# A Fourier transform fused into a leaky-ReLU MLP: moving the last chunk's sums to VectorE and splitting one weight conversion

## The chip, the cores and the metric

The kernel runs on one core of a Trainium2 chip. A core has five engines that each work through their own queue of instructions and wait for one another by semaphores: TensorE (matmuls, PE in the profile, with its weight loads as PEld), VectorE (DVE), ScalarE (ACT), GpSimd (POOL), and SyncE (SP), which here only issues transfers between HBM and the on-chip memory SBUF. TensorE writes its results to the eight banks of a second memory, PSUM. The metric is the time of one execution on the device in microseconds, taken as the median of three runs.

## The reference

```python
def _attn_ref(x):                       # x: (8, 3008, 256)
    X = np.fft.fft(x, axis=1)
    X = np.fft.fft(X, axis=2)
    return X.real.astype(np.float32)

def _moe_ref(x, w_in, w_out):           # x: (24064, 256), w_in: (256, 2048), w_out: (2048, 256)
    h = x @ w_in
    g = np.maximum(0.01 * h, h)
    return (g @ w_out).astype(np.float32)
```

The real part of a two-dimensional Fourier transform over sequence and features is taken for each of eight batches. Its 24064 rows then go through an MLP with a hidden layer of 2048 and a leaky ReLU. The weights are given in float64.

## The kernel before

Everything is computed in fp32. The transform along the features is folded into `w_in`, so that one set of weights `wf` stands for both. The transform along the sequence is made of sums and differences on VectorE and GpSimd (called folds) and a few matmuls with cosine and sine tables (`dft`, lines 489 to 524 and 691 to 701). Its result for one batch and one parity of the frequencies is a unit; there are 16 units. The float64 weights are turned into fp32 by bit operations (class `Weights`, lines 551 to 601). `begin` cuts out mantissa and exponent, `mantissa` (line 591, one VectorE instruction) adds the low word, and `end` (lines 600 and 601, two VectorE instructions) puts sign and exponent in. `w_out` comes in eight parts, o to o7.

The columns of the output are worked on in chunks. Two first pieces take a plain way (lines 881 to 931). The other columns make 31 chunks (t from 0 to 30), the class `Chunk`. A chunk of up to 378 pairs of columns goes through these stages:

- `up` (line 1090): for each of 16 blocks f of the hidden layer, one matmul into a cosine bank and one into a sine bank. ScalarE copies the cosine part (line 1099), VectorE makes sum and difference of the two (line 1106, a pair of instructions, which also empties the sine bank), and ScalarE applies the leaky ReLU (line 1360).
- The product with `w_out` is a block matrix product by a scheme with fewer multiplications. It has 28 sums of hidden blocks (`SUMS`, `Chunk.sum`, line 1123, one instruction of 128 x 752 numbers each), 18 sums of weights made once (`W_SUMS`, `sum_weights`, on GpSimd, line 661), 26 products of four matmuls each (`PRODUCTS`, line 1140; a matmul appears as two in the profile), and 34 combinations of the products (`COMBINED`, line 1184) on VectorE, some of them after ScalarE has copied a product out of PSUM (line 1156). Eight of the combinations are results, which SyncE stores.

The products go in turn into three banks, `sum_psa` to `sum_psc`. A product takes a bank only after the combinations that read its former content (`leave`, line 1168).

The order of the instructions on each engine is written out by `rest` (line 1272). It makes a list of events, each with a time in steps; a chunk has 16 steps, one for each block f, and the events are issued in the order of those times. Chunk t starts at step 16 t. Its ups come at 1.20 and on, its sum i at `SUMS_AT[i]`, and its products from step 18.1 on at 6.5 matmuls a step. So one chunk's products run beside the next chunk's ups, and after the last chunk's ups only its sums, products and combinations are left. At whole steps `start_work` issues other work, and the function `some` gives out folds and combinations from their queues, up to an amount that `now[0]` scales.

Ten sums of each chunk are on VectorE (`BY_VECTOR`) and 18 on GpSimd. In the last chunk the sums with i % 3 == 2 are on VectorE also, which makes 17 there and 11 on GpSimd:

```python
every[t].sum(i, nc.vector if i in BY_VECTOR or t == count - 1 and i % 3 == 2 else None)   # line 1346
```

A sum on GpSimd is given one more wait: `wait_for_gate` (line 990) makes it wait for the last instruction before it on VectorE that has both its operands in SBUF, although it uses no result of that instruction.

The last part of `w_out`, o7, is converted at step 2 of the first chunk, and the weight sums that read it follow:

```python
if r == 2:                      # line 1383
    convert_on(o7, None)        # mantissa, then end
    sum_weights(2)
    sum_weights(3)
```

Of the kernel before, what the change touches and what calls it, by code (L numbers as in the profile page):

```python
# [46 lines left out]
PLAIN = 2  # L47
EARLY = 14
FIRST_DOWN = 18.1
RF = 126  # L50
FIRST_SHARE = 1.0
DIRECT = (11, 13)
WORK_FROM = 14
FOLDS_FROM = 16
# [34 lines left out]
NA = 24  # L89

SUMS_AT = [14.51, 15.26, 16.05, 16.0, 16.74, 17.24, 17.74, 18.73, 18.48, 19.22, 19.47, 20.71, 20.32, 21.56, 22.06, 22.67, 22.04, 24.14, 24.64, 25.38, 25.37, 27.17, 27.22, 28.21, 29.08, 30.06, 30.17, 31.54]
UP_FROM, DOWN_FROM, PER_STEP, LATER = 1.20, 18.10, 6.5, 0
BY_VECTOR = (0, 3, 6, 8, 9, 12, 16, 17, 21, 25, )
ON_POOL, ON_VECTOR, AHEAD, X_AHEAD, TRANSFORM_FROM, TURNS = 1.20, 1.20, 1, 2, 8, 2
SLOTS, RS, SS, PARTS = 28, 191, 764, 24

# [184 lines left out]
def tile_fnet_leaky_relu(  # L281
# [15 lines left out]
    nc = tc.nc  # L297
# [137 lines left out]
    class Rows:  # L435
# [3 lines left out]
        def __init__(self, src, scratch, part, c):  # L439
            self.src, self.scratch, self.part, self.c = src[0:ROWS], scratch, part, c  # L440
            self.places = PLACES[c] if part else range(16)
# [170 lines left out]
    def convert_on(old, new):  # L612

        old.mantissa()
        if new is not None:
            new.begin()
        return old.end()
# [380 lines left out]
    class Slots:  # L998
# [3 lines left out]
        def __init__(self):  # L1002
            self.under = {SLOTS + i: {4 * RF * i // SS, (4 * RF * (i + 1) - 1) // SS} for i in range(16)}
            self.free = set(range(SLOTS)) - set().union(*self.under.values())
# [23 lines left out]
        def place(self, i, n):  # L1028
            if i >= SLOTS:
                return block_sb[:, (i - SLOTS) * 4 * RF : (i - SLOTS + 1) * 4 * RF].rearrange("p (g n) -> p g n", g=4)[:, :, 0:n]  # L1030
            return block_sb[:, i * SS : i * SS + 4 * RS].rearrange("p (g n) -> p g n", g=4)[:, :, 0:n]

        def row(self, r, g, n):
            if r[0] >= SLOTS:
                all_of = block_sb[:, 0 : 64 * RF].rearrange("p (i n) -> p i n", n=4 * RF)
                return all_of[:, r[0] - SLOTS : r[-1] + 1 - SLOTS, g * RF : g * RF + n]
            all_of = block_sb.rearrange("p (i n) -> p i n", n=SS)
# [206 lines left out]
    def work():  # L1244

        yield WORK_FROM, 0
        load_x(1, 0)
        yield FOLDS_FROM, 0  # L1250
        folds_of_x(0)
        for u in range(1, len(units) - 1):
            b, c = units[u]
            if c == 0:
                yield step_of(u, 0), 0
                load_x(b + 1, 1)
                yield 0, X_AHEAD
                folds_of_x(1)
                fold_halves_of_x()
                yield from transform(u + 1)  # L1260
            else:
                yield step_of(u, 0), 0
                if b + 1 < B:
                    load_x(b + 1, 0)
                    yield 0, X_AHEAD
                    folds_of_x(0)
                yield step_of(u, TRANSFORM_FROM), 0
                yield from transform(u + 1)

    every, waiting = [], []  # L1270

    def rest():

        count = len(chunk)
        every.extend(Chunk(t) for t in range(count))
        events = []
        for t in range(count):
            for f in range(NF):
                events.append((16 * t + UP_FROM + f, 3, t, f))
            for i, s in enumerate(SUMS_AT):  # L1280
                events.append((16 * t + s + LATER, 1, t, i))
            for m in range(4 * len(PRODUCTS)):
                events.append((16 * t + (DOWN_FROM if t else FIRST_DOWN) + m / PER_STEP, 2, t, m))
        for r in range(16 * count + 18):
            events.append((r + 0.01, 0, r // 16, r % 16))
        events.sort()
        rings["up"] = [0, [cos_ps[1], sin_ps[1]]]
        rings["sum"] = [0, sums_ps]
        rings["ev"], rings["e0"] = [0, [ev_sb]], [0, [e0_sb]]
        ups = [(t, f) for t in range(count) for f in range(NF)]  # L1290

        def seed(at):
            if at < len(ups):
                every[ups[at][0]].seed(ups[at][1])

        def seed_next(at):

            if at < EARLY:
                seed(at + 1)
            if at + 2 > EARLY:  # L1300
                seed(at + 2)

        us, now = [0.0, 0.0], [1.0]

        def some(pool):

            us[pool], us[1 - pool] = min(us[pool], 0.3) + (ON_VECTOR, ON_POOL)[pool] * now[0], us[1 - pool] - 100.0
            for part in every:
                part.make_some(us)
            folds.emit(us)  # L1310
            us[1 - pool] += 100.0

        todo, until, empty = work(), 0, -1

        def go_on(step):
            nonlocal until, empty
            while not folds.queue:
                if empty < 0:
                    empty = step
                if step < max(until, empty + after[0]):  # L1320
                    return
                got = next(todo, None)
                if got is None:
                    until = 10**6
                    return
                until, after[0] = got
                empty = -1

        after = [0]
        seed(0)  # L1330
        for _, kind, t, i in events:
            if kind == 0:
                start_work(16 * t + i)
                now[0] = FIRST_SHARE if 16 * t + i < 34 else 1.0
                if 0 < t < count:
                    rings["dft"] = [0, [misc_ps]]
                if t == count and waiting:
                    for to in waiting.pop():
                        nc.scalar.activation(to, to, ACT.Lrelu)
                go_on(16 * t + i)  # L1340
                some(1)
                if t >= count:
                    folds.emit_copies()
                    some(0)
            elif kind == 1:
                every[t].sum(i, nc.vector if i in BY_VECTOR or t == count - 1 and i % 3 == 2 else None)
            elif kind == 2:
                every[t].product(*divmod(i, 4))
                if t == count - 1:
                    for pool in (0, 1, 0, 1):  # L1350
                        some(pool)
            else:
                if i == 0 and t > 0 and every[t].u > every[t - 1].u:
                    assert t < 2 or transformed[0] >= every[t].u and not folds.queue, (t, transformed, len(folds.queue))
                part = every[t]
                made = part.up(i)
                seed_next(16 * t + i)
                folds.emit_copies()
                for to in sum(waiting, []):
                    nc.scalar.activation(to, to, ACT.Lrelu)  # L1360
                waiting[:] = [part.hidden(*made)]
                some(0)
        while any(part.open for part in every):
            some(0)
            some(1)
# [6 lines left out]
    def start_work(r):  # L1372


        if r == 0:
            convert_on(o6, o7)
        if r in PLAIN_UP:
            raised(*steps[PLAIN_UP[r]])
            activate(*steps[PLAIN_UP[r]], later=waiting)
        if r in PLAIN_DOWN:  # L1380
            at, half = PLAIN_DOWN[r]
            down_plain(*steps[at], halves=(half,))
        if r == 2:
            convert_on(o7, None)
            sum_weights(2)
            sum_weights(3)
        if r in (5, 7):
            part = (r - 5) // 2
            fold_halves(t, part, 0, slice(0, 2 * FI))
            evens.append(Direct(t[:, part, 0, :, part * P : (part + 1) * P], part, even_tables[part], 0))  # L1390
        if r in (8, 10):
            evens[(r - 8) // 2].fold_odd(t[:, (r - 8) // 2, 1, 0:2, 0:P])
        if r == 9:
            rings["dft"] = rings["up"]
            nyq_t = nyquist_tile()
            made = butterfly(nyquist_halves(nyq_t, 0), B, 0, 0)
            made[0](even_rows(nyq_of[0], B))
            made[1](odd_rows(nyq_of[0], B))
            store_nyquist(0, nyq_t)
            spread(1)  # L1400
        if r in DIRECT:
            dft_direct(DIRECT.index(r))
# [9 lines left out]
    with tc.manual_schedule(engines={mybir.EngineType.DVE, mybir.EngineType.PE, mybir.EngineType.SP}):  # L1412
        with tc.manual_schedule(engines={mybir.EngineType.Pool, mybir.EngineType.Activation}):
# [9 lines left out]
            t = xt[:, 0 : 8 * FI * D].rearrange("p (h m c d) -> p h m c d", h=2, m=2, c=2 * FI)  # L1423
# [85 lines left out]
        with tc.manual_schedule(engines={mybir.EngineType.Pool, mybir.EngineType.Activation}):  # L1509
# [35 lines left out]
            o6, o7 = load_w_out(6), load_w_out(7, now=False)  # L1545
# [61 lines left out]
```

## Time and profile before

| | |
|---|---|
| median of 3 runs | 1833.05 us (1833.03 to 1833.87) |
| the profiled execution's own time | 1834.63 us |
| its span, first to last instruction | 1832.8 us |
| TensorE busy | 1818.5 us, 99% |
| VectorE busy | 1546.2 us, 84% |
| ScalarE busy | 1124.6 us, 61% |
| GpSimd busy | 1101.7 us, 60% |
| mean granted TensorE clock | 0.998 |
| sums on GpSimd (line 1123) | 551, 1955 ns each on average |
| sums on VectorE (line 1123) | 317, 1299 ns each on average |

The profile is of one execution. A row of the timeline gives start, duration, engine, line, operation, what is written and read, the shape and the number of instructions, and in brackets how long the engine was idle before it and whose result ended that. "L1140" is a line of the code. A mean of a group mixes instructions that ran freely with those that stood still during their execution. The granted clock is the share of full speed that TensorE was allowed.

### The profile page before, as it was taken

Reading aid. Unit: us, or ns where it says so; the run is one execution under the profiler, and the core shown is the slowest. Engines: PE = TensorE matmul, PEld = TensorE weight load, DVE = VectorE, ACT = ScalarE, POOL = GpSimd, SP = SyncE. Lnnn points to the kernel's source line nnn. Section 1 sums busy time; section 2 is a strip of 40 time slices with the busy share of each in tenths; the row PEclk is TensorE's granted clock in tenths of the full one; section 3 lists DMA queues with packets and bytes.
Section 4 is the critical chain, followed back from the end, with each engine's and each line's share of the span. In section 5 each row is a group of like instructions: output and inputs, shape, how many; then the busy total and the mean of one; then the engine's idle time right before and its main releaser. Section 6 shows DMA issues by size and latency. Waiting matters only on the chain.

```text
span 1832.8 us, 27088 instructions
## 1 busy us (share of the span) xinstructions
PE 1818.5 (99%) x9424; PEld 1547.3 (84%) x9424; DVE 1546.2 (84%) x3212; ACT 1124.6 (61%) x2298; POOL 1101.7 (60%) x595
## 2 busy tenths in 40 slices
PE   9999999999999999999999999999999999999998
PEld 7887888888888888888888888888888888888887
DVE  8979898897888978899787988879898798788776
ACT  4558666675666756576565766557666675565650
POOL 0244666565666666666665666666566665766664
PEclk9999999999999999999999999999999999999999
DMA  6312021202102011021101112111021100100000
GB/s 235 118 39 98 28 70 34 72 14 68 33 28 72 23 63 30 29 70 35 63 18 54 46 33 72 33 53 30 28 70 35 65 16 30 27 30 18 14 9 30
DMA packets 65897, 88.61 MB, mean 48 GB/s; under 512 B 10064, under 2 KB 53456, under 8 KB 65760
## 3 DMA queue, kind: packets, MB, share of 16 engines
q1 hardware_dynamic: 65616, 86.88, 14.6%
q8 instruction: 74, 1.21, 0.3%
q14 instruction: 63, 0.52, 0.1%
q10 hardware_dynamic: 144, 0.00, 0.0%
HBM read 62.12 MB, written 24.72 MB: 47 GB/s over the span
## 4 chain that ended last, share of the span: by engine, by line
PE 96%; DVE 2%; POOL 1%; issue 1%; POOLq 0%; ACT 0%; DVEq 0%
PE sum_psc L1140 21%; PE sum_psa L1140 17%; PE sum_psb L1140 16%; PE cos_psa L1093 9%; PE sin_psa L1093 8%; PE cos_psb L1093 8%; PE sin_psb L1093 8%; PE dft_ps L699 3%; PE sum_psa L925 1%; PE dft_ps L925 1%; PE sum_psb L925 1%; PE sum_psc L925 1%; DVE part L1184 1%; PE sum_psa L1410 1%; POOL block L1123 1%
## 5 line engine op out<-in xcount | busy, mean ns | idle before, releaser
L1123 POOL TENSOR_TENSOR block<-block 128x752 f32<-128x752 f32 (+2 forms) x551 | 1070.0, 1955 | 638.8 <-DVE xt L946 178.7
L1360 ACT ACTIVATE block<-block 128x376 f32<-128x376 f32 (+5 forms) x718 | 426.4, 623 | 3.2 <-DVE block L1106 2.5
L1123 DVE TENSOR_TENSOR block<-block 128x752 f32<-128x752 f32 (+2 forms) x317 | 411.1, 1299 | 5.9 <-POOL block L1123 5.7
L1106 DVE TENSOR_TENSOR block<-cos,sin_psa 128x376 f32<-128x376 f32 (+2 forms) x510 | 250.9, 533 | 143.5 <-PE sin_psa L1093 139.9
L1140 PEld LDWEIGHTS sum_psc<-block,wt 128*128 128x128 f32 x1736 | 291.2, 190 | 47.1 <-issue 1.8
L1140 PE MATMUL sum_psc<-block,wt 128*128 128x188 f32 (+2 forms) x1736 | 329.2, 322 | 1.7 <-DVE part L1184 1.7
L1106 DVE TENSOR_TENSOR block<-cos,sin_psb 128x376 f32<-128x376 f32 (+2 forms) x482 | 240.2, 539 | 104.2 <-PE sin_psb L1093 103.0
L1140 PE MATMUL sum_psa<-block,wt 128*128 128x188 f32 (+2 forms) x1736 | 312.8, 321 | 0.4 <-POOL block L1123 0.4
L1140 PEld LDWEIGHTS sum_psa<-block,wt 128*128 128x128 f32 x1736 | 283.4, 189 | 23.5 <-POOL block L1123 0.7
L1099 ACT COPY cos<-cos_psa 128x376 f32<-128x376 f32 (+2 forms) x255 | 119.0, 467 | 250.6 <-PE cos_psa L1093 247.8
L1099 ACT COPY cos<-cos_psb 128x376 f32<-128x376 f32 (+2 forms) x241 | 113.6, 471 | 210.4 <-PE cos_psb L1093 210.3
L1093 PE MATMUL sin_psa<-mixs,wf 128*128 128x376 f32 (+2 forms) x510 | 199.9, 473 | 1.1 <-DVE block L1106 1.1
L1093 PE MATMUL cos_psa<-mixc,wf 128*128 128x376 f32 (+2 forms) x510 | 199.8, 473 | 0.5 <-ACT cos_psa L1088 0.5
L1184 DVE TENSOR_TENSOR part<-part 128x188 f32<-128x188 f32 (+2 forms) x465 | 189.8, 445 | 2.8 <-ACT part L1156 1.0
L1093 PE MATMUL sin_psb<-mixs,wf 128*128 128x376 f32 (+2 forms) x482 | 191.5, 479 | 0.0
L1093 PE MATMUL cos_psb<-mixc,wf 128*128 128x376 f32 (+2 forms) x482 | 191.4, 478 | 0.0
L1140 PE MATMUL sum_psb<-block,wo 128*128 128x188 f32 (+2 forms) x992 | 187.6, 321 | 0.0
L1140 PEld LDWEIGHTS sum_psb<-block,wo 128*128 128x128 f32 x992 | 165.3, 189 | 22.8
L1140 PEld LDWEIGHTS sum_psb<-block,wt 128*128 128x128 f32 x992 | 163.5, 189 | 22.8
L1140 PE MATMUL sum_psb<-block,wt 128*128 128x188 f32 (+2 forms) x992 | 176.8, 321 | 0.0
L1088 ACT ACTIVATE cos_psa<-nb,wn 128x376 f32<-128x376 f32 (+2 forms) x255 | 146.0, 572 | 8.4
L1093 PEld LDWEIGHTS sin_psa<-mixs,wf 128*128 128x128 f32 x510 | 96.4, 189 | 63.2 <-DVE block L1106 1.7
(212 smaller groups left out, 1954.3 us busy)
## 6 DMA issues: line engine op xcount, KB each, us to landing
xt<-in_x_dram SPq DMA_DIRECT2D x28, 1024.0 KB, 5.5
out_dram<-part SPq DMA_DIRECT2D x176, 94.0 KB, 1.7
out_dram<-part SPq DMA_DIRECT2D x64, 94.5 KB, 1.7
tabe<-in_seq_tab_dram SPq DMA_DIRECT2D x29, 190.0 KB, 2.5
nb<-nyq_dram SPq DMA_DIRECT2D x23, 188.0 KB, 3.8
block<-in_w_in_dram SPq DMA_DIRECT2D x8, 512.0 KB, 5.5
block<-in_w_out_dram SPq DMA_DIRECT2D x8, 512.0 KB, 4.6
xt<-in_first_x_dram SPq DMA_DIRECT2D x4, 768.0 KB, 8.2
```

The source lines that it names most:

```text
L699: nc.tensor.matmul(o, lhsT=still, rhs=moving, start=(i == 0), stop=(i == 3), skip_group_check=True)
L925: nc.tensor.matmul(sums[j][d][:, r * n : (r + 1) * n], lhsT=wo[:, fs[h] // 4, fs[h] % 4, d], rhs=a[r][h], start=(f == 0 and r == 0 and h = ...
L1088: nc.scalar.activation(cos_ps[self.half(f)][:, 0 : self.w], columns_of(nb_sb, self.u, self.j, self.w), ACT.Copy, scale=wn[:, f : f + 1])
L1093: nc.tensor.matmul(bank[:, 0 : self.w], lhsT=wf[:, i, f * P : (f + 1) * P], rhs=columns_of(mix_sb[i], self.u, self.j, self.w), start=(i == ...
L1099: nc.scalar.copy(copy, cos[:, 0 : self.w])
L1106: nc.vector.tensor_tensor(block.row(to, g, self.n), x, y, op=op)
L1123: ins = (engine or nc.gpsimd).tensor_tensor(self.value(16 + i), xa, ya, op=ALU.add if sign > 0 else ALU.subtract)
L1140: nc.tensor.matmul(to, lhsT=weight(w)[:, g], rhs=self.value(v)[:, g], start=(first and at == 0), stop=(last and g == 3), skip_group_check= ...
L1184: ins = nc.vector.tensor_tensor(part_of[self.copy[v]][:, 0:n], xa, ya, op=ALU.add if sign > 0 else ALU.subtract)
L1360: nc.scalar.activation(to, to, ACT.Lrelu)
L1410: nc.tensor.matmul(pt[:, 0:columns], lhsT=blank[:, 0:P], rhs=blank[:, 0:columns], start=True, stop=True)
```

## The change

- In the last chunk (t = 30) all 28 sums are on VectorE, the eleven of GpSimd included (`LAST_ON_POOL` is empty). In the other chunks `ON_GPSIMD` is the complement of the former `BY_VECTOR`: nothing moves.
- The last chunk's sums are issued one step sooner, but those that were due after step 17.05 not before that point, and those that were due before it at their old place.
- The conversion of o7 is split. Its `mantissa` is issued at step 1 of the first chunk, its `end` at step 3, with the weight sums that follow.
- The amount that `some` gives out is scaled by 0.9 before step 34 and by 1.2 from there to step 48; it was 1.0.
- `LATER` (which was 0) goes, and `FIRST_PER` has the value of `PER_STEP`.

```diff
-FIRST_SHARE = 1.0
+FIRST_PER = 6.5
+O7_AT = (1, 3)
+SHARES = (0.9, 1.2)
...
-UP_FROM, DOWN_FROM, PER_STEP, LATER = 1.20, 18.10, 6.5, 0
-BY_VECTOR = (0, 3, 6, 8, 9, 12, 16, 17, 21, 25, )
+UP_FROM, DOWN_FROM, PER_STEP = 1.20, 18.10, 6.5
+ON_GPSIMD = (1, 2, 4, 5, 7, 10, 11, 13, 14, 15, 18, 19, 20, 22, 23, 24, 26, 27)
+LAST_ON_POOL = ()
+LAST_SOONER = 1.0
...
             for i, s in enumerate(SUMS_AT):
-                events.append((16 * t + s + LATER, 1, t, i))
+                events.append((16 * t + (s if t < count - 1 else max(s - LAST_SOONER, min(s, 17.05))), 1, t, i))
             for m in range(4 * len(PRODUCTS)):
-                events.append((16 * t + (DOWN_FROM if t else FIRST_DOWN) + m / PER_STEP, 2, t, m))
+                events.append((16 * t + (DOWN_FROM + m / PER_STEP if t else FIRST_DOWN + m / FIRST_PER), 2, t, m))
...
-                now[0] = FIRST_SHARE if 16 * t + i < 34 else 1.0
+                now[0] = SHARES[0] if 16 * t + i < 34 else SHARES[1] if 16 * t + i < 48 else 1.0
...
-                every[t].sum(i, nc.vector if i in BY_VECTOR or t == count - 1 and i % 3 == 2 else None)
+                every[t].sum(i, None if i in (LAST_ON_POOL if t == count - 1 else ON_GPSIMD) else nc.vector)
...
-        if r == 2:
-            convert_on(o7, None)
+        if r == O7_AT[0]:
+            o7.mantissa()
+        if r == O7_AT[1]:
+            o7.end()
             sum_weights(2)
             sum_weights(3)
```

## The prediction

> **What bounds the kernel now.** I read the busy row first, then TensorE's idle time in order of time, then the engines that end it, last the granted clock.
>
> ```profile
> PE 1818.5 (99%) x9424; PEld 1547.3 (84%) x9424; DVE 1546.2 (84%) x3212; ACT 1124.6 (61%) x2298; POOL 1101.7 (60%) x595
> ```
>
> TensorE sets the time; a change is worth what it gives back of the 14.3 us in which TensorE isn't busy, and of any time at a lower clock. The waits by window leave three places: about 103 us, 181 to 189 us, and the last 41 us. From 192 to 1776 us TensorE shows no wait at all. TensorE in the tail (start, duration, what, idle before it):
>
> ```profile
> 1790.67 1.44 PE L1140 MATMUL sum_psb<-block,wo 128*128 128x188 f32 x8
> 1795.66 2.87 PE L1140 MATMUL sum_psc<-block,wo 128*128 128x188 f32 x8 [3.56 <-POOL block L1123]
> 1798.33 4.45 PE L1140 MATMUL sum_psc<-block,wt 128*128 128x188 f32 x16
> ...
> 1813.38 1.54 PE L1140 MATMUL sum_psa<-block,wt 128*128 128x188 f32 x8 [0.40 <-POOL block L1123]
> ...
> 1826.49 1.54 PE L1140 MATMUL sum_psc<-block,wo 128*128 128x188 f32 x8
> ```
>
> Eight matmuls normally take 1.275 us from start to start, so the group at 1795.66 was due at 1791.95. Besides the 3.7 us of waiting, its own eight take 2.67 and the next sixteen 4.29 instead of 2.55: half speed. The same stretch by windows (PE, PEld, DVE, ACT, POOL, then the granted clock):
>
> ```profile
> 1792.00:1796.00 4.00, 0.44 (x2) 0.34 (x2) 1.98 (x3) 0.54 (x2) 4.00 (x2) 0.88 0.17 55
> 1796.00:1804.00 8.00, 8.00 (x33) 8.00 (x33) 5.79 (x3) 0.00 (x0) 5.52 (x3) 0.63 0.00 0
> ```
>
> A mean of 0.88 over 4 us is 0.97 us at one half, 0.63 over 8 us is 5.9: the clock was halved for 6.9 us, from 1795.03, 2.9 us after TensorE stopped. Why GpSimd was late, from its row and VectorE's:
>
> ```profile
> 1791.60 9.93 POOL L1123 TENSOR_TENSOR block<-block 128x752 f32<-128x752 f32 x4 [6.82 <-DVE part L1184]
> ```
> ```profile
> 1788.05 1.79 DVE L1123 TENSOR_TENSOR block<-block 128x752 f32<-128x752 f32 x2
> ...
> 1791.34 2.64 DVE L1123 TENSOR_TENSOR block<-block 128x752 f32<-128x752 f32 x3
> 1797.38 5.79 DVE L1123 TENSOR_TENSOR block<-block 128x752 f32<-128x752 f32 x3 [3.40 <-POOL block L1123]
> ```
>
> The sum that the matmuls wait for is put on GpSimd behind an artificial wait on VectorE's combinations (6.82 us), then stands 4.0 us (the chain shows it until 1795.62) because VectorE's three sums run until 1793.98. At the front, VectorE, then TensorE:
>
> ```profile
> 97.44 0.74 DVE L1106 TENSOR_TENSOR block<-cos,sin_psa 128x250 f32<-128x250 f32 x2 [1.35 <-PE sin_psa L1093]
> ...
> 100.37 0.69 DVE L591 SCALAR_TENSOR_TENSOR wo<-block,wo 128x512 f32<-128x512 uint32 x1
> 100.97 0.69 DVE L600 SCALAR_TENSOR_TENSOR block<-block 128x512 int32<-128x512 int32 x1
> 101.69 0.69 DVE L601 SCALAR_TENSOR_TENSOR wo<-wo,block 128x512 f32<-128x512 f32 x1
> 102.30 0.73 DVE L1106 TENSOR_TENSOR block<-cos,sin_psa 128x250 f32<-128x250 f32 x2
> ```
> ```profile
> 101.41 0.58 PE L1093 MATMUL cos_psa<-mixc,wf 128*128 128x250 f32 x2
> 103.09 0.69 PE L1093 MATMUL sin_psa<-mixs,wf 128*128 128x250 f32 x2 [1.10 <-DVE block L1106]
> ```
>
> The three conversion instructions stand ahead of the L1106 pair that must empty sin_psa before TensorE may fill it again. Of the third place the waits (total, times, longest) show:
>
> ```profile
> PE sum_psc L1140 <- DVE part L1184: 1.7, 1, 1.7
> ...
> PE sum_psa L1140 <- DVE part L1184: 0.6, 1, 0.6
> ```
>
> Two products, at 184.79 and 188.63, wait for VectorE to read the bank that they take; VectorE is behind with its whole queue there.
>
> [...] a VectorE sum takes 0.93 us alone, but 1.6 to 2.5 us beside GpSimd's. [...] Here the drop came after 2.9 us and lasted 6.9. [...]
>
> **The change part by part.** (1) The last chunk's eleven GpSimd sums go to VectorE. They add 11 x 0.855 = 9.4 us there (0.855 is the start-to-start time of sums in the rows at 1788.05 and 1791.34). GpSimd then has nothing after its last sum of chunk 29, which ends by 1782.3 (its row of three begins at 1778.78)[...]. What it can give TensorE: from 1790.67 to 1826.49 it started 176 matmuls, worth 28.05 us of 35.82. So 7.77 us are lost: 3.71 waiting, 3.13 half clock, 0.66 around 1813.38, 0.27 before 1826.49.
>
> Now VectorE's own lateness. From the L1106 pair that starts at 1780.08 (released by TensorE, so not earlier), the new order has 4 L1106 x 0.46 + 12 sums x 0.855 + 15 combinations x 0.265 = 1.84 + 10.26 + 3.98 = 16.08 us up to sum 11, which product 7 reads; some four instructions that wait for their own predecessor add 0.1 each, the pipeline end 0.08. That is 1796.6. Product 7 is due three groups after 1791.95, at 1795.77. So TensorE waits about 0.8 us there, far below the 2.9 us at which the clock fell. After it VectorE makes a sum in 0.855 us against TensorE's 1.275 per product; laid out in the same way, the following products find their sums over 1 us early. Product 4, the one late today, needs sum 7 and the bank that two combinations free at about 1792.0: no cost beyond 0.1. Net: 7.77 - 0.8 = 7.0 us.
>
> (2) "One step sooner" (a step is some 3.4 us of TensorE) costs nothing by itself: it moves sums ahead of combinations of chunk 29 on VectorE. Queued behind them are L1184 combinations that free banks; that lateness is the 0.1 above. It has bounds of 0 and 1.0. The end is as before: six combinations and the last stores follow the last matmul.
>
> (3) The conversion. L591 now stands after L901, that is in VectorE's 1.35 us of idle before 97.44; its 0.69 us is covered (without that cover it would push the pair by 0.6). L600 and L601 come after the second L1106 pair, which then runs at 100.37 and ends at 101.1; the matmul due at 101.83 (0.42 after 101.41) doesn't wait. Gain 1.26, plus 0.10 by which the next group is late today: 1.36. Late next: the third pair, behind L600/L601 until about 102.4, whose matmul comes four microseconds on (107.43 today). The weight sums on GpSimd wait for L601, which ends at 102.4 as it does now; no matmul before 142 us reads them.
>
> (4) The shares. 0.9 before step 34 and 1.2 up to step 48 move some forty VectorE instructions and ten ScalarE ones by about one step, with four groups of four L699 matmuls, and one table load on SP's queue behind three output stores (under 4 us later; its readers come later still). The first moved one stands at 191.5 us, the last at 267, so the 0.53, 1.66 and 0.56 us of waits at 181 to 189 us keep their order and stay. Where it acts TensorE has no wait to lose, so nothing can be gained; VectorE is full from 192 to 215 and from 240 to 270 (22.51 of 23.00, 29.96 of 30.00 us), so work put off can make TensorE wait. Today's closest calls there leave about 1 us. Bounds 0 and +2; I take 0.1. FIRST_PER, the removed LATER and the complement list move nothing.
>
> Sum: 7.0 + 1.36 - 0.1 = 8.3 us off the span of 1832.8. The profiled execution took 1834.63 and the median of the runs is 1833.05; I take the same difference off the median: 1824.8.
>
> **The rivals.** (a) The front gains nothing, because the second L1106 pair is held by L900/L901 (the row before L591): 1826.1. Against it: L901 ends at 100.45, TensorE is due at 101.83. (b) The postponed folds make TensorE wait 2 us between 192 and 270: 1826.8. For it: VectorE's full windows; against: slack of a microsecond. (c) VectorE becomes the tail's bound. If sums take the tail's mean of 1.19 us (20 of 752 columns, 23.3 us) instead of 0.93, sum 11 is 12 x 0.26 = 3.1 us later, TensorE idles 3.9 and the clock halves again: 7.77 - 3.9 - 3.1 = 0.8, with the front 1831.0, no change to be measured. It begins at 2.9 us of idle, 1.11 us per sum. [...] (d) Slower: the same place, with every sum at the 2.0 us[...]. 12 x 1.07 + 0.8 = 13.6 us of idle and 3.1 of half clock lose 9.0 more than is freed: 1840.7. It is slower by over 0.2% from 1.67 us per sum. Only work left on GpSimd could do that, and none is.
>
> **How the numbers follow.** My forecast has a chance of 0.76 and its own range of 1823.2 to 1826.2 (nothing late at product 7, or up to 2 us late there). (a) 0.08, (b) 0.11, (c) 0.03, (d) 0.02. The range 1823.2 to 1827.6 takes in (a) and (b). A measurement of this kernel tells 0.2%, 3.7 us, from no change: the forecast, (a) and (b) are faster, 0.95; (c) the same, 0.03; (d) slower, 0.02.
>
> **What would show it.** No GpSimd row after about 1781 us; no TensorE idle over 1 us and a granted clock of 1.00 to the end; a short wait on VectorE L1123 at the eighth product; no wait at the third sin_psa near 101.8; the waits at 181 to 189 us still there, 1.4 us sooner. It is wrong if TensorE waits over 2.9 us anywhere in the tail, or new waits show between 192 and 270 us.

## The result, and the profile after

| | before | after |
|---|---|---|
| median, measured side by side | 1833.11 us (1832.99 to 1833.87, 6 runs) | 1826.11 us (1825.96 to 1826.50, 6 runs) |
| the profiled execution's own time | 1834.63 us | 1826.21 us |
| its span | 1832.8 us | 1824.4 us |

The ratio of after to before is 0.9962, with a 95% interval from 0.9949 to 0.9974. The change makes the kernel 7.0 us faster. The forecast was 1824.8 us with a range from 1823.2 to 1827.6, so the time is inside the range and 1.3 us above the forecast. The two profiled executions differ by 8.4 us in span, where the forecast's sum was 8.3; the medians differ by only 7.0. Part of what follows is about that missing 1.4 us.

In the changed kernel the lines concerned stand four further down: sums are L1127, products L1144, combinations L1188, the pair of sum and difference L1110, the three conversion instructions L595, L604 and L605.

First the busy row of the page of after (busy us, share of the span, instructions):

```profile
PE 1814.5 (99%) x9424; PEld 1543.8 (85%) x9424; DVE 1551.8 (85%) x3223; ACT 1125.0 (62%) x2298; POOL 1077.3 (59%) x584
```

VectorE has eleven instructions more and GpSimd eleven fewer, as the change says. TensorE is busy 4.0 us less for the same 9424 matmuls: that isn't less work, but the half-speed stretch that is gone, 3.13 us by the forecast's working, and 0.9 us that wasn't traced further.

TensorE in the tail of after (start, duration, what, idle before it), from the group that came just ahead of the long wait of before:

```profile
1789.09 1.44 PE L1144 MATMUL sum_psb<-block,wo 128*128 128x188 f32 x8
1790.63 1.54 PE L1144 MATMUL sum_psc<-block,wo 128*128 128x188 f32 x8
1792.01 2.71 PE L1144 MATMUL sum_psc<-block,wt 128*128 128x188 f32 x16
1795.10 1.54 PE L1144 MATMUL sum_psc<-block,wo 128*128 128x188 f32 x8 [0.38 <-DVE block L1127]
...
1818.14 1.44 PE L1144 MATMUL sum_psc<-block,wo 128*128 128x188 f32 x8
```

From 1789.09 to the start of the last group there are 29.05 us, for the same 176 matmuls that took 35.82 us before. At the full pace they are worth 28.05, so 1.0 us of loss is left where there were 7.77. The 1.0 is 0.27 before the group at 1790.63, 0.54 before the one at 1795.10 (0.38 of it labelled), and 0.10 in each of these two groups themselves. The 3.56 us wait, the 0.40 us wait further on and the half-speed groups are gone. The windows of after (PE, PEld, DVE, ACT, POOL, then the granted clock) say the same of the clock, which was 0.88 and 0.63 in these two stretches before:

```profile
1792.00:1796.00 4.00, 3.62 (x23) 3.33 (x22) 4.00 (x6) 0.00 (x0) 0.00 (x0) 1.00 0.22 71
1796.00:1804.00 8.00, 8.00 (x53) 8.00 (x52) 8.00 (x16) 0.63 (x2) 0.00 (x0) 1.00 0.00 0
```

GpSimd's last row of after, and then VectorE's rows where the sums stand:

```profile
1773.88 4.83 POOL L1127 TENSOR_TENSOR block<-block 128x756 f32<-128x756 f32 x2 [1.25 <-DVE part L1188]
```
```profile
1786.56 3.49 DVE L1127 TENSOR_TENSOR block<-block 128x752 f32<-128x752 f32 x4
...
1791.55 6.91 DVE L1127 TENSOR_TENSOR block<-block 128x752 f32<-128x752 f32 x8
```

GpSimd ends at 1778.7 and never comes back. Eight sums in a row take 6.91 us, which is 0.855 from start to start: VectorE works at the undisturbed pace that the forecast used, and during the row of eight it is the engine that TensorE is waiting for.

The front, VectorE and then TensorE of after:

```profile
95.86 0.69 DVE L595 SCALAR_TENSOR_TENSOR wo<-block,wo 128x512 f32<-128x512 uint32 x1
97.23 0.74 DVE L1110 TENSOR_TENSOR block<-cos,sin_psa 128x250 f32<-128x250 f32 x2 [0.69 <-PE sin_psa L1097]
...
100.53 0.73 DVE L1110 TENSOR_TENSOR block<-cos,sin_psa 128x250 f32<-128x250 f32 x2
101.18 0.70 DVE L604 SCALAR_TENSOR_TENSOR block<-block 128x512 int32<-128x512 int32 x1
```
```profile
101.20 0.58 PE L1097 MATMUL cos_psa<-mixc,wf 128*128 128x250 f32 x2
101.62 0.58 PE L1097 MATMUL sin_psa<-mixs,wf 128*128 128x250 f32 x2
102.04 1.01 PE L891 MATMUL cos_psb<-mixc,wf 128*128 128x251 f32 x4
```

In before the last of these rows was:

```profile
103.61 1.01 PE L887 MATMUL cos_psb<-mixc,wf 128*128 128x251 f32 x4
```

L595 stands in what was idle time: the idle before the pair at 97.23 fell from 1.35 to 0.69 us, by about the length of the instruction. L604 and L605 come after the second pair, and the matmul at 101.62 follows 0.42 us after the one before it, with no wait. After was 0.21 us ahead at the `cos_psa` group (101.41 and 101.20) and is 1.57 us ahead at the last row: a gain of 1.36 us.

The waits of TensorE in after (total us, times, longest) are otherwise those of before:

```profile
PE sum_psc L1144 <- DVE part L1188: 1.7, 1, 1.7
...
PE sum_psa L1144 <- DVE part L1188: 0.6, 1, 0.6
...
PE sum_psc L1144 <- DVE block L1127: 0.4, 1, 0.4
```

Setting the two traces side by side, matmul by matmul, gives the account of the spans. After is 0.21 us ahead from 20 us on, from a start-up that differs from profile to profile (0.40 us ahead of before in the conversion alone, 0.38 behind in the shares alone) and that no part of the forecast counted; 1.26 more comes at the `sin_psa` matmul that stood at 103.09 and 0.10 at the next one; 0.01 between there and 1790 us; and 6.77 between 1795 us and the end. That is 8.35 us, the distance of the last groups (1826.49 and 1818.14). Between 190 and 240 us, where the shares of the queues were changed, after loses up to 1.0 us of its lead several times and is back each time by the end of the step. The windows of that stretch (same columns) show that TensorE stays without a gap, as it was before, although VectorE is all but full in the first and the last of them:

```profile
192.00:215.00 23.00, 23.00 (x126) 19.86 (x125) 22.93 (x46) 16.43 (x38) 14.70 (x9) 1.00 0.16 46
215.00:240.00 25.00, 25.00 (x136) 21.48 (x135) 21.77 (x47) 13.73 (x27) 15.14 (x8) 1.00 0.28 92
240.00:270.00 30.00, 30.00 (x155) 25.43 (x154) 29.54 (x58) 20.10 (x41) 20.13 (x11) 1.00 0.11 33
```

### The profile page after: what moved, and what is told of

Same layout as the page of the kernel before. It is cut to its first block, busy times and chain, and to the rows that moved or that the text cites. A ratio compares the mean times of both kernels' runs of the same rounds, so it can differ in the third digit from the quotient of the medians.

```text
span 1824.4 us, 27085 instructions
## 1 busy us (share of the span) xinstructions
PE 1814.5 (99%) x9424; PEld 1543.8 (85%) x9424; DVE 1551.8 (85%) x3223; ACT 1125.0 (62%) x2298; POOL 1077.3 (59%) x584
## 4 chain that ended last, share of the span: by engine, by line
PE 96%; DVE 3%; issue 0%; DMA 0%; ACT 0%; POOL 0%; DVEq 0%
PE sum_psc L1144 21%; PE sum_psa L1144 17%; PE sum_psb L1144 17%; PE cos_psa L1097 9%; PE sin_psa L1097 9%; PE sin_psb L1097 8%; PE cos_psb L1097 8%; PE dft_ps L703 3%; PE sum_psa L929 1%; PE dft_ps L929 1%; PE sum_psb L929 1%; PE sum_psc L929 1%; DVE block L1127 1%; DVE part L1188 0%; DVE block L1110 0%; PE sin_psb L891 0%
## 5 line engine op out<-in xcount | busy, mean ns | idle before, releaser
L1127 POOL TENSOR_TENSOR block<-block 128x752 f32<-128x752 f32 (+2 forms) x540 | 1045.6, 1948 | 615.3 <-DVE xt L950 173.4
L1127 DVE TENSOR_TENSOR block<-block 128x752 f32<-128x752 f32 (+2 forms) x328 | 416.3, 1273 | 0.2
L1110 DVE TENSOR_TENSOR block<-cos,sin_psa 128x376 f32<-128x376 f32 (+2 forms) x510 | 250.9, 533 | 141.0 <-PE sin_psa L1097 137.4
L1144 PEld LDWEIGHTS sum_psc<-block,wt 128*128 128x128 f32 x1736 | 289.3, 189 | 47.1 <-issue 1.8
L1144 PE MATMUL sum_psc<-block,wt 128*128 128x188 f32 (+2 forms) x1736 | 327.2, 321 | 1.7 <-DVE part L1188 1.7
L1110 DVE TENSOR_TENSOR block<-cos,sin_psb 128x376 f32<-128x376 f32 (+2 forms) x482 | 240.1, 539 | 101.4 <-PE sin_psb L1097 100.3
L1144 PE MATMUL sum_psa<-block,wt 128*128 128x188 f32 (+2 forms) x1736 | 312.1, 321 | 0.0
L1144 PEld LDWEIGHTS sum_psa<-block,wt 128*128 128x128 f32 x1736 | 283.5, 189 | 22.8
L1188 DVE TENSOR_TENSOR part<-part 128x188 f32<-128x188 f32 (+2 forms) x465 | 188.9, 443 | 3.3 <-ACT part L1160 1.4
L1144 PE MATMUL sum_psb<-block,wo 128*128 128x188 f32 (+2 forms) x992 | 188.0, 321 | 0.0
L1144 PEld LDWEIGHTS sum_psb<-block,wo 128*128 128x128 f32 x992 | 165.2, 189 | 22.8
L1144 PEld LDWEIGHTS sum_psb<-block,wt 128*128 128x128 f32 x992 | 163.5, 189 | 22.8
L1144 PE MATMUL sum_psb<-block,wt 128*128 128x188 f32 (+2 forms) x992 | 176.9, 321 | 0.0
```

Source lines behind the costliest of these rows:

```text
L1110: nc.vector.tensor_tensor(block.row(to, g, self.n), x, y, op=op)
L1127: ins = (engine or nc.gpsimd).tensor_tensor(self.value(16 + i), xa, ya, op=ALU.add if sign > 0 else ALU.subtract)
L1144: nc.tensor.matmul(to, lhsT=weight(w)[:, g], rhs=self.value(v)[:, g], start=(first and at == 0), stop=(last and g == 3), skip_group_check= ...
L1188: ins = nc.vector.tensor_tensor(part_of[self.copy[v]][:, 0:n], xa, ya, op=ALU.add if sign > 0 else ALU.subtract)
```

## The experiments

Each was timed against the kernel before on the same chip. The first four share 34 runs of the kernel before (median 1833.21, 1831.69 to 1834.61), the last four share 15 (median 1833.35, 1831.81 to 1834.58). The change itself was timed beside a third set (median 1833.11), so a difference between two changed kernels can be off by a few tenths of a microsecond, an estimate from these three medians. None of the kernels leaves work out.

### The kernel before, once more

No edit. The question is where the 1.4 us between spans and medians went.

> The kernel before, unchanged, to see its executions beside each other. Theory A (the profiled execution of before lost more in the tail than a usual one, because TensorE's clock falls at a moment that varies): the time is 1833.1 us within 0.3, the spans are about 1831.3 us in most runs, 1.5 below the 1832.8 of the profile of before, and a profile of such a run shows fewer than 6.9 us at half clock or a shorter wait before the product of sum 7. Theory B (the front or the middle of the kernel differs between executions): a new profile shows the same tail, 3.56 us of waiting and 6.9 us at half clock, and the difference lies before 1776 us. Theory C (the loss lies outside the span): all spans are 1832.8 us.

Measured: 1833.25 us (1832.81 to 1834.61, 13 runs), ratio 1.0003 (0.9995 to 1.0011). Its profiled execution took 1833.25 us with a span of 1831.5. TensorE in its tail, and the windows:

```profile
1795.84 2.87 PE L1140 MATMUL sum_psc<-block,wo 128*128 128x188 f32 x8 [3.54 <-POOL block L1123]
1798.51 2.88 PE L1140 MATMUL sum_psc<-block,wt 128*128 128x188 f32 x16
1801.22 1.44 PE L1140 MATMUL sum_psc<-block,wo 128*128 128x188 f32 x8
```
```profile
1792.00:1796.00 4.00, 0.46 (x3) 0.17 (x2) 2.16 (x3) 0.54 (x2) 4.00 (x2) 0.93 0.22 69
1796.00:1804.00 8.00, 8.00 (x42) 8.00 (x43) 6.06 (x4) 0.32 (x1) 5.70 (x3) 0.82 0.00 0
```

The wait is the same (3.54 us against 3.56), and so are the eight slow matmuls after it. But the next sixteen take 2.71 us to the following start (1798.51 to 1801.22) instead of 4.29: the clock is back after 3.4 us, not after 6.9 (0.07 x 4 + 0.18 x 8 = 1.7 us of clock lost in the two windows, against 0.12 x 4 + 0.37 x 8 = 3.4 in the first profile). Up to there the two traces of one and the same kernel keep their distance, and then this one gains 1.6 us, as theory A said. So the time at half clock has two lengths in these two executions, 3.4 and 6.9 us by the windows, and the execution that I forecast from had the long one.

Two kernels further down keep the long wait, and the matmuls after it show the same two lengths. The first eight took 2.67 us in before, in this run and in the shares alone, and 2.66 in the conversion alone: half speed in all four. The next sixteen, worth 2.55, took 4.29 us in before and 4.03 in the conversion alone, but 2.71 here and 2.83 in the shares alone. What decides between the long and the short half clock isn't shown by these four executions.

The 34 runs of before fit this. They lie in three groups with gaps between them: seven at 1831.69 to 1832.02, fifteen at 1832.86 to 1833.57, twelve at 1833.85 to 1834.61. All twelve of the last group have a mean clock of 0.998, all others 0.999; 3.4 us more at half clock take 3.4 x 0.5 / 1832 = 0.0009 off the mean. The medians of the two upper groups are 1.2 us apart, somewhat less than the 1.6 between the traces. What parts the first two groups wasn't settled, since no trace of the fastest group was taken.

### The last chunk alone

```diff
-O7_AT = (1, 3)
-SHARES = (0.9, 1.2)
+O7_AT = (2, 2)        # conversion as before
+SHARES = (1.0, 1.0)   # shares as before
```

> All 28 sums of the last chunk on VectorE one step sooner, with the conversion of o7 whole at step 2 and the shares at 1.0. Theory A: about 5.7 us faster than before by the medians (7.0 by the sum of the prediction, less the 1.3 us by which the profiled execution lost more than usual). Theory B: 7.0 us faster, and the shortfall is in the front. In both the wait of 1.10 us near 103 us stays.

Measured: 1827.69 us (1827.56 to 1827.93, 6 runs), ratio 0.9970 (0.9959 to 0.9981), 5.5 us faster than before. Its waits of TensorE still hold the one at the front and have the short one of the tail:

```profile
PE sin_psa L1097 <- DVE block L1110: 1.1, 1, 1.1
...
PE sum_psc L1144 <- DVE block L1127: 0.4, 1, 0.4
```

In the traces the last chunk's part is worth 6.77 us against the long half clock; against the short one that is 6.77 - 1.6 = 5.2. The 5.5 of the medians lie between, near the latter, and not at the 7.0 of the forecast. The six runs of this kernel spread over 0.4 us. Six are few, but the 11 runs of a kernel further down that has no long wait either spread over 0.8 us, and 13 runs of each kernel that keeps the wait over 1.8 to 2.5: the scatter goes with the wait.

### The conversion alone

```diff
-SHARES = (0.9, 1.2)
+SHARES = (1.0, 1.0)
...
-LAST_ON_POOL = ()
-LAST_SOONER = 1.0
+LAST_ON_POOL = (1, 4, 7, 10, 13, 15, 18, 19, 22, 24, 27)
+LAST_SOONER = 0.0
```

> Only the split of the conversion of o7, with shares of 1.0 and the tail as before. The prediction and theory A: 1.3 us faster, no wait on the third L1106 pair near 102 us, everything after it 1.4 us sooner. Theory B: between 0 and 0.3 us faster, since the wait comes back later, at 134 or at 184 us.

Measured: 1832.16 us (1831.25 to 1833.11, 13 runs), ratio 0.9994 (0.9985 to 1.0002). The gain of 1.05 us in the medians is below what the interval can tell from nothing, since the tail of before with its scatter is still there. The trace tells it better. TensorE at the front of this kernel:

```profile
101.01 0.58 PE L1097 MATMUL cos_psa<-mixc,wf 128*128 128x250 f32 x2
101.43 0.58 PE L1097 MATMUL sin_psa<-mixs,wf 128*128 128x250 f32 x2
101.85 1.01 PE L891 MATMUL cos_psb<-mixc,wf 128*128 128x251 f32 x4
```

The wait of 1.10 is gone. This kernel is 0.40 us ahead of before at the first of these rows (101.41 before) and 1.76 at the last (103.61 before): again 1.36 us. Among runs of the same mean clock, 0.998, the median is 1832.70 us (5 runs) against 1834.31 of before (12 runs), 1.6 us less. From the other side, the kernel with the last chunk alone is 1.58 us slower than the full change by the medians (1827.69 - 1826.11), and that holds the shares too. The forecast's 1.36 stands.

### The shares alone

```diff
-O7_AT = (1, 3)
+O7_AT = (2, 2)
...
-LAST_ON_POOL = ()
-LAST_SOONER = 1.0
+LAST_ON_POOL = (1, 4, 7, 10, 13, 15, 18, 19, 22, 24, 27)
+LAST_SOONER = 0.0
```

> Only the shares of 0.9 and 1.2, conversion and tail as before. The prediction: the same time within 0.2 us, no new wait of TensorE between 192 and 270 us. The rival of the prediction (postponed folds): up to 2 us slower.

Measured: 1833.86 us (1832.10 to 1834.55, 13 runs), ratio 1.0001 (0.9993 to 1.0009). The median is 0.65 us above that of before, and the interval of the ratio reaches from 1.3 us below it to 1.6 above (0.0007 and 0.0009 of 1833), so no effect is shown, and the runs leave room for one of up to 1.6 us. Much of the 0.65 can be the mix of half clocks: seven of these 13 runs have the mean clock of 0.998, against 12 of the 34 of before, and among those the medians are 1834.38 and 1834.31. The forecast's 0.1 can be neither confirmed nor told from nothing. Its trace has no wait of TensorE that before doesn't have; groups of `dft` matmuls (L699 before) come earlier or later among the others, which moves single matmuls by up to a microsecond and is made good within the step: it is 0.38 us behind before both ahead of this stretch and after it.

### The sums on VectorE, but not sooner

```diff
-LAST_SOONER = 1.0
+LAST_SOONER = 0.0
```

> The changed kernel with the last chunk's sums all on VectorE, but at their old times (not a step sooner). Theory L ([...] the engine is what matters): sum 11 comes later on VectorE, TensorE waits about 1.1 us for it instead of 0.4, and the time is 1826.4 to 1827.2 us. Theory S (being sooner is what matters): most of the tail's gain is gone, 1830 us or more.

Measured: 1826.76 us (1826.45 to 1827.12, 5 runs), ratio 0.9965 (0.9952 to 0.9978): 0.65 us slower than the change. TensorE in its tail:

```profile
1791.87 1.54 PE L1144 MATMUL sum_psc<-block,wo 128*128 128x188 f32 x8 [1.17 <-DVE block L1127]
```

With the sums at their old places in the list, the product that was late before is still late, by 1.2 instead of 3.6 us; the wait in the middle of the tail goes. The time is in the range of theory L, but the wait isn't where it was expected: none shows before the product that reads sum 11. From 1793.25 on the matmuls take 2.55 us for sixteen, the full pace, and the mean clock of the profiled run is 1.0. So the other engine alone is enough to keep TensorE away from half speed.

### Sooner, but on GpSimd

```diff
-LAST_ON_POOL = ()
+LAST_ON_POOL = (1, 4, 7, 10, 13, 15, 18, 19, 22, 24, 27)
```

> The changed kernel with the eleven sums of the last chunk back on GpSimd, but issued a step sooner as in the change. Theory L: waits of TensorE for GpSimd's sums come back (about 1 us before product 4 and 3 to 4 us before a later one), with a half clock after the longer; the time is 1830 to 1832.5 us, of which the front's 1.3 us are the larger part of the gain. Theory S: 1826 to 1827.5 us, as the change.

Measured: 1828.71 us (1828.46 to 1829.28, 11 runs), ratio 0.9976 (0.9967 to 0.9985), 4.6 us faster than before and 2.6 slower than the change. It lies between the two expectations, so neither theory had it right. TensorE, VectorE and GpSimd in its tail:

```profile
1791.94 1.51 PE L1144 MATMUL sum_psc<-block,wo 128*128 128x188 f32 x8 [0.83 <-DVE part L1188]
...
1797.05 1.54 PE L1144 MATMUL sum_psc<-block,wo 128*128 128x188 f32 x8 [1.05 <-DVE block L1127]
...
1802.03 2.79 PE L1144 MATMUL sum_psb<-block,wt 128*128 128x188 f32 x16 [0.89 <-DVE block L1127]
```
```profile
1792.77 9.11 DVE L1127 TENSOR_TENSOR block<-block 128x752 f32<-128x752 f32 x5
```
```profile
1788.12 2.35 POOL L1127 TENSOR_TENSOR block<-block 128x752 f32<-128x752 f32 x1 [4.35 <-DVE block L1127]
1792.93 2.41 POOL L1127 TENSOR_TENSOR block<-block 128x752 f32<-128x752 f32 x1 [2.46 <-DVE part L1188]
```

Sums on both engines take longer beside each other: five sums on VectorE take 9.11 us (1.8 each, against 0.86 in the change), and one on GpSimd 2.4 (1.78 for its later ones). But a step earlier, the sum that is needed is begun at 1788.12 and not at 1791.60, and the lateness comes in three pieces of about a microsecond. None of them reaches the 2.9 us at which the clock fell in before, and the mean clock of the profiled run is 1.0, so nothing is paid twice. Starting sooner alone thus removes the long wait and the half clock; moving the engine gives another 2.6 us on top of it.

### GpSimd kept busy in the tail

The change, with a GpSimd sum of the same size beside each of the last chunk's sums from the fifth on. Its operands are a buffer that nothing reads any more; it has to wait for nothing and nobody waits for it. The question is whether VectorE's sums stay at 0.93 us, and the time at 1826.1, beside a GpSimd at work.

```diff
                 every[t].sum(i, None if i in (LAST_ON_POOL if t == count - 1 else ON_GPSIMD) else nc.vector)
+                if t == count - 1 and i > 3:
+                    nc.gpsimd.tensor_tensor(xt[:, 0:752], xt[:, 752:1504], xt[:, 1504:2256], op=ALU.add)
```

> The changed kernel, and beside the last chunk's sums from the fifth on GpSimd gets 24 additions of 128 x 752 numbers on the tile xt, which nothing reads any more: the computed output is the same. [...] single sums take 1.5 to 2.6 us instead of 0.93, TensorE waits 1 to 4 us in all in the tail, and the time is 1 to 6 us over the change's 1826.1.[...]

Measured: 1858.51 us (1858.36 to 1860.47, 4 runs), ratio 1.0143 (1.0126 to 1.0160): 32.4 us slower than the change, where I had expected a few. GpSimd, VectorE and TensorE in its tail:

```profile
1778.52 53.01 POOL L1352 TENSOR_TENSOR xt<-xt 128x752 f32<-128x752 f32 x24
```
```profile
1788.35 7.45 DVE L1188 TENSOR_TENSOR part<-part 128x189 f32<-128x189 f32 x4
...
1805.44 0.60 DVE L1188 TENSOR_TENSOR part<-part,sum_psc 128x189 f32<-128x189 f32 x2
1805.96 6.94 DVE L1188 TENSOR_TENSOR part<-part 128x189 f32<-128x189 f32 x4
1812.83 19.50 DVE L1127 TENSOR_TENSOR block<-block 128x752 f32<-128x752 f32 x8
```
```profile
1796.41 2.85 PE L1144 MATMUL sum_psb<-block,wt 128*128 128x188 f32 x8 [8.57 <-DVE part L1188]
1800.72 2.87 PE L1144 MATMUL sum_psb<-block,wo 128*128 128x188 f32 x8 [1.47 <-DVE block L1127]
...
1815.39 2.87 PE L1144 MATMUL sum_psc<-block,wt 128*128 128x188 f32 x8 [4.09 <-DVE block L1127]
```

Eight sums take 19.50 us, 2.4 each. Worse hit are the small combinations: four take 7.45 us, 1.9 each, where a row of four combinations takes 1.15 us in the change. The 1.9 is near the 1.78 us that a GpSimd sum of this size takes undisturbed in before (at 1819.01), though the combination itself takes 0.35; that each of them stood for the length of one GpSimd instruction is my estimate from these figures. The slow instructions of VectorE have both operands in SBUF, as GpSimd's have; why they slow each other the traces don't show. It isn't GpSimd's work as such that slows VectorE: the two combinations at 1805.44, which read one operand from PSUM, take 0.60 us with GpSimd at work beside them, as they do in the change (0.61). The waits shown add up to 22.5 us between 1787 and 1833 (8.57, 1.47, 2.50, 4.09, 4.40, 0.66, 0.83), and the matmuls at half speed lose about 9 more (six groups of eight at 1.3 us or so each, one of sixteen at about 1.4), together the 32 us.

### A version that is faster than both

What the change leaves is one wait of 0.5 us in the tail and two at 183 to 187 us. This one puts sum 12 half a step later, behind the sums that the next products need, and gives the first chunks' folds and products a slightly different beat.

```diff
-EARLY = 14
-FIRST_DOWN = 18.1
+EARLY = 13
+FIRST_DOWN = 18.25
...
-SHARES = (0.9, 1.2)
+SHARES = (0.75, 1.3)
...
-                events.append((16 * t + (s if t < count - 1 else max(s - LAST_SOONER, min(s, 17.05))), 1, t, i))
+                events.append((16 * t + (s if t < count - 1 else max(s - LAST_SOONER, min(s, 17.05)) + (0.5 if i == 12 else 0.0)), 1, t, i))
```

> The changed kernel with four small edits: sum 12 of the last chunk half a step later, so that sum 11, which a product waits for, comes before it on VectorE; shares of 0.75 and 1.3; the first chunk's products from step 18.25 on (18.1); one step fewer (13 for 14) in which the first chunk uses one pair of banks. By the theory of the tail the wait of 0.38 us before product 7 goes: 0.4 to 0.5 us. The other edits aim at the waits of 0.5 us at 134 us and of 1.66 and 0.55 us at 183 to 187 us and should take between 0.3 and 1.2 us from them. Sum: 1824.5 to 1825.5 us. If VectorE is merely behind by the same work, the waits at 183 to 187 only move and the time is 1825.6 us.

Measured: 1824.15 us (1823.87 to 1824.29, 4 runs), ratio to before 0.9952 (0.9937 to 0.9967), 2.0 us below the change and 0.35 below the expected range. Of TensorE's waits for sums (L1127) and combinations (L1188) one is left in its whole profile:

```profile
PE sum_psa L1144 <- DVE part L1188: 1.2, 1, 1.2
```

The waits of 1.66 and 0.55 us near 183 and 187 have become this one of 1.17, and the tail has none that the profile labels. How the 2.0 us divide among the four edits wasn't tried.

## Why the prediction was right, and where it was off

**The last chunk.** Right in mechanism and in size against its own execution: 7.77 us lost before, 1.0 left, 6.77 gained where the sum had 7.0. The wait came at the eighth product, as forecast. TensorE came to it 0.9 us later than at full pace (1795.10 - 1789.09 - 4 x 1.275), where I had worked out 0.8; only 0.54 of that is the wait itself, since product 4, which I put at no more than 0.1, was late by 0.27 already and its group by another 0.1. The rate of 0.855 us per sum held over the row of eight. One reading was loose: of the 4.0 us for which the GpSimd sum of before stood, 1.78 are what such a sum takes undisturbed, so 2.2 of them came on top beside VectorE's sums. How much of the long wait was this and how much the artificial wait ahead of it stays open, since no run takes away the one and keeps the other.

What the forecast left out is what its second edit can do. It gave the whole gain to the change of engine and priced "one step sooner" as a cost only, of nothing within bounds of 0 and 1.0. The runs show that either edit alone avoids the half clock. With the conversion and the shares as in the change, the engine alone gives 6.6 of the 7.2 us that lie between 1833.35 and the change's 1826.11, and starting sooner alone 4.6; both figures hold the front's 1.4, and the rest overlaps, so they can't be added. On top of the engine, starting sooner is worth 0.65 us.

**The conversion.** 1.36 forecast, 1.26 + 0.10 = 1.36 in both traces, 1.58 by the medians of two kernels that differ in it and the shares. Its cover is where the forecast said: the idle before the first L1110 pair.

**The shares.** 0.1 forecast within bounds of 0 and 2; nothing shows in the trace, and the runs can't tell 0.1 from nothing.

**The step that failed: "I take the same difference off the median".** The 8.3 us was worked out from one execution, and 3.13 us of it was half clock of the long kind. The median run of before has the short kind, as the profile of a run at 1833.25 us shows, and loses 1.6 us less; in the tail of after there is no half clock before the last matmul, so its profiled execution (1826.21) and its median (1826.11) agree. Taking 8.3 - 1.6 = 6.7 off the median of 1833.05 gives 1826.4, and 1826.11 was measured. That the time still lies inside the forecast's narrower range, by 0.1 us, is luck: that width was left for lateness at product 7. The sign was to be seen beforehand: the profiled execution of before, 1834.63, lay 1.6 us above the median of the runs shown and above the slowest of them (1833.87), and its table of windows, with 6.9 us at half clock, showed a place where it could have lost more than they.

**The rivals.** (a), that the front gains nothing, gave 1826.1, which is the time measured to the tenth; it is nevertheless wrong, since the trace shows the front's 1.36 us. (b), a new wait between 192 and 270 us, gave 1826.8 and is wrong too: TensorE is busy without a gap in that stretch. A time alone would have confirmed (a) and could hardly have told (b) apart. (c) is out, since the sums ran at 0.86 and not at 1.19 us: with no sum on GpSimd, VectorE's took what they take alone. (d) named work left on GpSimd as the only thing that could turn the change into a loss. Put there, it does so, at 1858.51 us. Its price of 1840.7 was too low by 18 us, because it counted slowed sums alone, at the 2.0 us that one took beside GpSimd in before (at 1783.58), where they took 2.4; the combinations, which took 1.84 us on average in place of 0.35, weren't in it. Nor was a half clock that lasts through a row of waits: each group of eight matmuls from 1796.41 to 1822.66 took 2.54 to 2.88 us in place of 1.44.

## What to carry to other kernels

The stop of TensorE of 3.5 us was paid for twice here, and the second payment, the half clock after it, was of 3.4 us in one execution of the same kernel and of 6.9 in another: before a profiled difference is taken off a median, see which of the two lengths that execution had, and compare its own time with the other runs'. For the last stage of a pipeline, where no other work covers a late operand, ask both when the operand is begun and on which engine: either edit alone removed the long stop here, and the engine gave more. If VectorE and GpSimd would share such a stage with two-operand instructions in SBUF, price the short instructions at more than their own length too: here a combination of 0.35 us took 1.84 beside GpSimd's sums, and a VectorE sum of 0.93 took 2.4. A time that agrees with a story is weak evidence when several stories lie within a microsecond of each other; the wait that the story names has to be there or gone in the trace.

## What the runs showed of the hardware that was not expected

- After a stop of 3.5 us TensorE's clock was halved for 3.4 us in one profiled execution of before and for 6.9 us in another, with the same wait in both (3.54 and 3.56 us). It fell 2.9 us after TensorE had stopped in the one with 6.9 us, and about 3.1 us after it in the other, by the windows.
- With waits in a row, in the kernel with GpSimd busy, six groups of eight matmuls took 2.54 to 2.88 us in place of 1.44, from 1796.41 to 1825.33, although the waits just ahead of two of them were of 1.47 and 2.50 us only. The profiled run's mean clock was 0.99.
- A VectorE combination of 0.35 us with both operands in SBUF took 1.84 us on average (8 of them) beside a GpSimd engine that works on without pause, though the two share no data. With one operand in PSUM two of them took 0.60 us there, as they do in the change (0.61).
